# Gelu straight from PSUM in the second phase, and a block's first products behind all reads of their tile

## Chip, cores and metric

The kernel runs on one core of a Trainium2 chip. The metric is the device time of one execution in microseconds. Before the change three runs took 1274.23, 1276.29 and 1277.38 us (median 1276.29).

## The reference

For 8 batches of 576 tokens with model width 512 three things follow one another, all in float32. First, attention in chunks of 64 tokens with 8 heads of 64. Second, a feed-forward layer with a residual; third, a gated layer that mixes tokens:

```python
x = x + relu(layernorm(x, eps=1e-6) * g_ln @ w_ch1) @ w_ch2          # 512 -> 2048 -> 512
h = gelu_tanh(x @ w_in)                                              # 512 -> 1024
u, v = h[..., :512], h[..., 512:]
v_n = (v - mean(v)) / sqrt(var(v) + 1e-6) * g_ln
v_s = einsum('ts,bsd->btd', w_sg, v_n) + b_sg[None, :, None]         # 576 x 576 over tokens
out = x + (u * v_s) @ w_out
```

Gelu is `0.5 * h * (1 + tanh(c * (h + 0.044715 * h**3)))`.

## The kernel before

The 4608 tokens are 36 tiles of 128. A float32 product is made of three float16 products: each operand is split into a high and a low half, scaled by a power of two, and low times low is left out.

**First phase: attention and the feed-forward layer.** Its instructions are collected by a `Plan`. Every `op` names its engine, a planned duration, what it reads and writes (by keys such as `P1` or by buffers), a priority and a latency that its readers on other engines see. `Plan.run` then plays the engines against each other and emits the instructions in the order that comes out; on the chip each engine runs its own list in that order. The keys only set the order. What really waits for what is found out afterwards from the tiles that the emitted instructions touch.

Tokens go through the feed-forward layer in blocks of two tiles. From block 4 on (14 blocks) a block has eight steps j. `ff1p` makes the hidden units of a step on banks 2 and 3; `ff2p` multiplies them by the second matrix by a scheme with seven products, P1 to P7, each a sum over the eight steps. P1 and P6 lie in one bank of the two-bank tile `pair0`, P5 and P7 in its other bank, P2 and P3 in `bank6`, P4 in `bank7`. TensorE takes them in the order 1, 6, 5, 7, 2, 3, 4. The step behind a block's last hidden step is two `ff1p` later, so between the last products of a block and the first of the next lies one `ff1p` (24 matmuls). After the last step (`j == 7`) ScalarE copies P1 and P5, scaled, into the buffers `u`, VectorE evicts P6, P7, P2, P3 and P4, and POOL adds the parts together; then the block's two tiles are stored.

**Second phase: the gated layer.** It works by hand-written order, with four groups of nine tiles. A *unit* is one output tile of TensorE: `v_unit` (one token tile, 512 columns of v), `u_unit` (128 rows of u by 384 tokens), `s_unit` (the mixing over tokens), `o_unit` (a token tile of the output). Each takes the next of four PSUM banks:

```python
def nb():
    rot[0] += 1
    return bank[rot[0] % 4]
```

A unit first issues its matmuls, then `tick()`, which issues what earlier units have put off with `later(k, fn)`: `fn` is issued at the k-th tick from there. So gelu of unit n is spread: its first ScalarE passes and the first VectorE pass (L1024) are issued in unit n, the tanh at the tick of unit n+1, and the last VectorE pass (`last`, L1031) at the tick of unit n+2. For v, statistics, normalisation and the split into halves follow over further ticks.

Group 0 begins with its nine v_units, followed by twelve u_units. For groups 0 to 2 the order is u_units, two sets of four s_units, and then this stage, which mixes the next group's v_units with this group's o_units:

```python
for c in "v0 v1 v2 v3 o0 v4 o1 v5 o2 v6 o3 v7 v8 o4 o5 o6 o7 o8".split():
```

In the same stage the gated u is split into halves (`split`, L247 to L249), and its scale is found by a maximum over all partitions (`fin_g`, `turn`, `spread`).

Of the kernel before, what the change touches and what calls it, by code (L numbers as in the profile page):

```python
# [10 lines left out]
F32 = mybir.dt.float32  # L11
# [4 lines left out]
ALU = mybir.AluOpType  # L16
# [116 lines left out]
def fused_kernel(ctx: ExitStack, tc, qkv, w1, w2, g1, w_in, w_out, wsgt, wsgs, g2, b_sg, out):  # L133
# [38 lines left out]
    e2g, i2g = (small.tile([P, 4], F32, name=f"{n}2g") for n in "ei")  # L172
    g1s = small.tile([P, 4], F32, name="g1s")
# [500 lines left out]

    def ff2p(b, j):
# [19 lines left out]
        for p in (1, 6, 5, 7, 2, 3, 4):  # L695
            op("PE", 326, lambda p=p: mm(p), rd=[h, f"w2_{j}"], wr=[f"P{p}"] + extra, prio=1000 + nff[0])
        if j == 7:
# [8 lines left out]
            def stt(p, c, out, add, n=0):  # L706
                op("DVE", 480, lambda: nc.vector.scalar_tensor_tensor(  # L707
                    out=out(), in0=POS[p][0], scalar=c, in1=add(), op0=ALU.mult, op1=ALU.add
                ), rd=[f"P{p}", f"P{3 if p == 2 else p}"], wr=u if n else [x1 if p == 4 else x0], prio=-120, lat=1200)

            def copy(p, c, n):
                op("ACT", 380, lambda: nc.scalar.activation(
                    out=U(n), in_=POS[p][0], func=AF.Copy, scale=c
                ), rd=[f"P{p}", f"P{p + 5 if p == 1 else 7}"], wr=[u[n // 2]], prio=-120, lat=1200 if n else 300)

            def add(x, d, v, ns):
                op("POOL", ns, lambda: nc.gpsimd.tensor_tensor(  # L717
                    out=d(), in0=d(), in1=v(), op=ALU.add
                ), rd=u, wr=[x], prio=-50)

            copy(1, ca, 0)
            stt(6, cb, lambda: U(1), lambda: U(0), 1)
            copy(5, cb, 2)
            stt(7, cb, lambda: U(3), lambda: U(1), 3)
            stt(2, ca, lambda: half(x0, 0), lambda: half(x0, 0))
            stt(3, ca, lambda: half(x0, 1), lambda: half(x0, 1))
            stt(4, cn, lambda: half(x1, 0), lambda: half(x1, 0))
            add(x0, lambda: x0.t, lambda: u[0].t, 1250)
            add(x1, lambda: half(x1, 0), lambda: U(3), 700)
            add(x0, lambda: half(x0, 1), lambda: U(2), 700)  # L730
            add(x1, lambda: half(x1, 1), lambda: U(3), 700)
            add(x1, lambda: half(x1, 1), lambda: U(2), 700)
# [102 lines left out]
    def x2_cols(g0, n):  # L835

        e, inv = e2g[:, g0:g0 + n], i2g[:, g0:g0 + n]
        top2(e, inv)
        nc.vector.tensor_scalar_mul(inv, inv, 2.0 ** 14)
        nc.vector.tensor_scalar(out=e, in0=e, scalar1=col("win_c"), scalar2=None, op0=ALU.mult)  # L840

# [30 lines left out]
    with tc.manual_schedule():  # L872
# [144 lines left out]
        def gelu(g, ps, n, o, done=None):  # L1017

            h = pb.tile([P, 512], F32, tag="h", name="h", bufs=4)[:, :n]
            q = pb.tile([P, 512], F32, tag="q", name="q", bufs=4)[:, :n]  # L1020
            nc.scalar.activation(out=h, in_=ps, func=AF.Copy, scale=e2g[:, g:g + 1])
            nc.scalar.activation(out=q, in_=h, func=AF.Square, scale=GA)  # L1022
            tick()
            nc.vector.scalar_tensor_tensor(out=q, in0=q, scalar=1.0, in1=h, op0=ALU.add, op1=ALU.mult)  # L1024

            def tanh():
                nc.scalar.activation(out=q, in_=q, func=AF.Tanh, scale=GC)
                later(1, last)

            def last():  # L1030
                nc.vector.scalar_tensor_tensor(out=o, in0=q, scalar=1.0, in1=h, op0=ALU.add, op1=ALU.mult)  # L1031
# [5 lines left out]
        def v_unit(g, i):  # L1037
# [9 lines left out]
            def stats():  # L1047
# [7 lines left out]
                    out=rs, in0=mv[:, 1:2], scalar1=z, scalar2=4e-6 * z, op0=ALU.mult, op1=ALU.add  # L1055
# [37 lines left out]
        def s_unit(g, e, m):  # L1093
# [48 lines left out]
            def fin_g3():  # L1142
# [6 lines left out]
                    out=col(f"c5_{e}"), in0=e_, scalar1=col("wout_c"), scalar2=None, op0=ALU.mult  # L1149
# [132 lines left out]
```

## Time and profile before

| | before |
|---|---|
| median of 3 runs | 1276.29 us |
| profiled execution | 1274.01 us |
| its span, first to last instruction | 1272.2 us |
| TensorE busy | 1218.5 us (96%) |
| VectorE busy | 825.1 us (65%) |
| ScalarE busy | 586.5 us (46%) |
| POOL busy | 491.2 us (39%) |
| mean granted TensorE clock | 0.993 |

The second phase begins at 867 us. A timeline names the tiles by the program's names: `pair` is `pair0`, `pb` one of the second phase's banks, `u` the buffers of the block's end. "Idle before" is the time that the engine stood still ahead of an instruction, with what ended it. An instruction of VectorE or ScalarE may start a little before the one ahead has ended, so starts that follow each other are closer than the durations.

### The profile page before, as it was taken

Reading aid. Unit: us, or ns where it says so; the run is one execution under the profiler, and the core shown is the slowest. Engines: PE = TensorE matmul, PEld = TensorE weight load, DVE = VectorE, ACT = ScalarE, POOL = GpSimd, SP = SyncE. Lnnn points to the kernel's source line nnn. Section 1 sums busy time; section 2 is a strip of 40 time slices with the busy share of each in tenths; the row PEclk is TensorE's granted clock in tenths of the full one; section 3 lists DMA queues with packets and bytes.
Section 4 is the critical chain, followed back from the end, with each engine's and each line's share of the span. In section 5 each row is a group of like instructions: output and inputs, shape, how many; then the busy total and the mean of one; then the engine's idle time right before and its main releaser. Section 6 shows DMA issues by size and latency. Waiting matters only on the chain.

```text
span 1272.2 us, 26588 instructions
## 1 busy us (share of the span) xinstructions
PE 1218.5 (96%) x11119; PEld 872.5 (69%) x11119; DVE 825.1 (65%) x1621; ACT 586.5 (46%) x963; POOL 491.2 (39%) x446
## 2 busy tenths in 40 slices
PE   6889999988999999999999999999999999999998
PEld 4677654667888888888888888884544554554553
DVE  7885125995766656555555665546979579669665
ACT  5775402545834533333334333535736626526530
POOL 3341401644656544434444344233434144233220
PEclk9999999989999999999999999999999999999999
DMA  9954002246312221222132120612030331331102
GB/s 303 261 172 120 1 26 67 74 149 181 101 51 68 51 73 48 66 67 67 52 67 60 51 59 18 156 28 91 9 68 33 116 59 42 125 59 42 50 1 75
DMA packets 106392, 102.05 MB, mean 80 GB/s; under 512 B 79648, under 2 KB 79648, under 8 KB 106272
## 3 DMA queue, kind: packets, MB, share of 16 engines
q1 hardware_dynamic: 106272, 100.36, 28.2%
q8 instruction: 87, 1.43, 0.5%
q14 instruction: 33, 0.27, 0.1%
HBM read 62.59 MB, written 18.87 MB: 64 GB/s over the span
## 4 chain that ended last, share of the span: by engine, by line
PE 75%; DVE 14%; ACT 3%; DMA 3%; POOL 2%; issue 2%; SPq 0%; DVEq 0%; ACTq 0%; POOLq 0%
PE bank L640 20%; PE pair L689 11%; PE bank L689 8%; PE pb L1105 8%; PE pb L1087 7%; PE pb L1167 6%; PE pair L557 3%; PE pb L1043 3%; PE bank L536 3%; PE bank L557 2%; DMA straw<-in_w 2%; DVE gl L249 1%; PE pair L295 1%; DVE tf L600 1%; PE pb L1106 1%
## 5 line engine op out<-in xcount | busy, mean ns | idle before, releaser
L640 PE MATMUL bank<-xT,w1h 128*128 128x256 f16 x1792 | 301.6, 273 | 0.0
L689 PEld LDWEIGHTS <-arena 128*128 128x128 f16 x2352 | 226.7, 98 | 46.0 <-issue 17.0
L640 PE MATMUL bank<-xT,w1l 128*128 128x256 f16 x896 | 245.0, 273 | 0.0
L669 POOL TENSOR_TENSOR arena<-arena 128x896 f16<-128x896 f32 x69 | 130.2, 1886 | 255.6 <-ACT arena L667 255.5
L667 ACT ACTIVATE arena<-arena 128x896 f16<-128x896 f32 x112 | 106.3, 949 | 204.7 <-PE bank L689 131.4
L640 PEld LDWEIGHTS <-w1h 128*128 128x128 f16 x1792 | 175.3, 98 | 21.7 <-issue 0.5
L662 DVE TENSOR_TENSOR arena<-arena 128x256 f32<-128x256 f32 x112 | 63.6, 568 | 149.1 <-ACT arena L655 146.9
L655 ACT ACTIVATE arena<-bank 128x512 f32<-128x512 f32 x112 | 66.6, 595 | 123.7 <-PE bank L640 122.5
L689 PE MATMUL pair<-w2s,arena 128*128 128x256 f16 x672 | 110.6, 274 | 10.3 <-DVE u L707 6.8
L689 PE MATMUL pair<-w,arena 128*128 128x256 f16 x672 | 111.0, 274 | 2.7 <-DVE u L707 1.3
L1119 POOL TENSOR_TENSOR uT<-uT,vs 128x512 f32<-128x512 f32 x32 | 49.0, 1533 | 151.6 <-DVE vs L1115 151.6
L1043 PE MATMUL pb<-win,x2T 128*128 128x512 f16 x432 | 96.8, 379 | 1.5 <-DVE x L707 1.5
L640 PEld LDWEIGHTS <-w1l 128*128 128x128 f16 x896 | 87.9, 98 | 10.4
L1087 PE MATMUL pb<-x2T,win 128*128 128x384 f16 x576 | 94.6, 326 | 0.0
L689 PE MATMUL bank<-w,arena 128*128 128x256 f16 x672 | 93.7, 274 | 0.0
L536 PE MATMUL bank<-xT,w1h 128*128 128x256 f16 x512 | 86.1, 273 | 6.7 <-DVE latel L541 2.9
L1105 PE MATMUL pb<-wsg,vh 128*128 128x512 f16 x288 | 88.0, 380 | 0.0
L1167 PE MATMUL pb<-wout,gh 128*128 128x512 f16 x288 | 85.7, 379 | 1.9 <-DVE x L1172 1.9
L1087 PEld LDWEIGHTS <-win 128*128 128x128 f16 x576 | 56.2, 98 | 37.5
L717 POOL TENSOR_TENSOR x<-x,u 128x256 f32<-128x256 f32 (+1 forms) x60 | 64.4, 1089 | 44.3 <-ACT arena L667 30.8
L1024 DVE SCALAR_TENSOR_TENSOR q<-q,h 128x384 f32<-128x384 f32 (+1 forms) x84 | 51.3, 614 | 39.0 <-ACT q L1022 39.0
L1043 PEld LDWEIGHTS <-x2T 128*128 128x128 f16 x432 | 41.3, 98 | 50.9 <-issue 2.7
(225 smaller groups left out, 2332.5 us busy)
## 6 DMA issues: line engine op xcount, KB each, us to landing
straw<-in_w SPq DMA_DIRECT2D x16, 1023.8 KB, 6.6
qkl<-in_qkv SPq DMA_DIRECT2D x26, 512.0 KB, 3.8
x2d<-x SPq DMA_DIRECT2D x36, 256.0 KB, 2.0
x<-x2d SPq DMA_DIRECT2D x36, 256.0 KB, 4.4
out<-x SPq DMA_DIRECT2D x36, 256.0 KB, 2.0
vl<-in_qkv SPq DMA_DIRECT2D x26, 256.0 KB, 2.7
qk<-in_qkv SPq DMA_DIRECT2D x10, 512.0 KB, 5.7
raw<-in_w_in SPq DMA_DIRECT2D x4, 1023.8 KB, 5.6
```

What stands on the lines that cost most here:

```text
L536: nc.tensor.matmul(acc, lhsT=w[j][:, k, fc], rhs=xT.t[:, x, k], start=(n == 0), stop=(n == 11))
L557: nc.tensor.matmul(acc[i], lhsT=h[x].t[:, c], rhs=w2t[j][:, f % 2, y], start=(f == 0 and n == 0), stop=(f == NF - 1 and n == 2),)
L640: nc.tensor.matmul(acc[:, y * 256:y * 256 + 256], lhsT=w[j][:, k, fc], rhs=xT.t[:, x, k], start=(n == 0), stop=(n == 11),)
L655: op("ACT", 600, lambda: nc.scalar.activation(out=o.t[:, 0:4].rearrange("p n t -> p (n t)"), in_=acc, func=AF.Relu, scale=0.5), rd=[kb] + ...
L667: op("ACT", 950, lambda: nc.scalar.activation(out=h.t[:, 0], in_=o.t[:, 1:8], func=AF.Copy), rd=[o] + ar, wr=[h], prio=-100)
L669: op(lo[0], lo[1], lambda: lo[2].tensor_tensor(out=h.t[:, 1], in0=o.t[:, 1:8], in1=h.t[:, 0], op=ALU.subtract), rd=[o], wr=[h], prio=-100)
L689: nc.tensor.matmul(acc, lhsT=h.t[:, x, n], rhs=r(y), start=(first and j == 0 and m == 0), stop=(j == 7 and m == 2), skip_group_check=True,)
L717: op("POOL", ns, lambda: nc.gpsimd.tensor_tensor(out=d(), in0=d(), in1=v(), op=ALU.add), rd=u, wr=[x], prio=-50)
L1043: nc.tensor.matmul(ps, lhsT=x[:, k, c], rhs=w[:, k, 512:1024], start=(n == 0), stop=(n == 11))
L1087: nc.tensor.matmul(ps, lhsT=w[:, k, fc], rhs=x[:, k, c], start=(n == 0), stop=(n == 11))
L1105: nc.tensor.matmul(ps, lhsT=v[:, fc], rhs=w[:, 0:512], **f)
L1167: nc.tensor.matmul(ps, lhsT=x[:, k, c], rhs=w[:, k], start=(n == 0), stop=(n == 11))
```

## The change

In the first phase the first products of a new block take the tile's other products as written too (`OWN`), for `j == 0`. The reads at the block's end get keys of their own (`q1`, `q6`, `q7`, `q5`), the eviction of P7 stands ahead of the copy of P5 and no longer behind it, planned latencies of 1200 ns are dropped to the default, and planned durations of the copies and of POOL's additions are raised.

In the second phase gelu no longer makes a scaled copy `h` of the products in SBUF. Square, the first VectorE pass and the last one read the bank `ps` itself. The scale of h moves into columns: `eg` holds, for each group, the scales of Square and tanh and the eps of the layer norm, which five more small operations in `x2_cols` work out, and the scale that u has kept goes into the column `c5` of the output.

```diff
--- before.py
+++ after.py
@@ -170,6 +170,7 @@
     diag = small.tile([4, 4], F32, name="diag")
     redg = small.tile([P, 4], F32, name="redg")
     e2g, i2g = (small.tile([P, 4], F32, name=f"{n}2g") for n in "ei")
+    eg = small.tile([P, 3, 4], F32, name="eg")
     g1s = small.tile([P, 4], F32, name="g1s")
     g2s = small.tile([P, 4], F32, name="g2s")
     bb = small.tile([P, S], F32, name="bb")
@@ -672,6 +673,8 @@
 
         return rest
 
+    OWN = {1: ["P6", "P5", "P7"], 2: ["P3"]}
+
     def ff2p(b, j):
 
         nff[0] += 1
@@ -693,7 +696,7 @@
 
         extra = ["pair0", "bank7", "scr0", "scr1", "scr2"] if (b, j) == (B0, 0) else []
         for p in (1, 6, 5, 7, 2, 3, 4):
-            op("PE", 326, lambda p=p: mm(p), rd=[h, f"w2_{j}"], wr=[f"P{p}"] + extra, prio=1000 + nff[0])
+            op("PE", 326, lambda p=p: mm(p), rd=[h, f"w2_{j}"], wr=[f"P{p}"] + extra + OWN.get(p, []) * (j == 0), prio=1000 + nff[0])
         if j == 7:
             x0, x1 = x_t.pop(2 * b), x_t.pop(2 * b + 1)
 
@@ -703,33 +706,33 @@
 
             U = lambda n: u[n // 2].t[:, n % 2 * 256:n % 2 * 256 + 256]
 
-            def stt(p, c, out, add, n=0):
+            def stt(p, c, out, add, x, rd=()):
                 op("DVE", 480, lambda: nc.vector.scalar_tensor_tensor(
                     out=out(), in0=POS[p][0], scalar=c, in1=add(), op0=ALU.mult, op1=ALU.add
-                ), rd=[f"P{p}", f"P{3 if p == 2 else p}"], wr=u if n else [x1 if p == 4 else x0], prio=-120, lat=1200)
-
-            def copy(p, c, n):
-                op("ACT", 380, lambda: nc.scalar.activation(
+                ), rd=[f"P{p}", *rd], wr=[x], prio=-120)
+
+            def copy(p, c, n, rd, wr):
+                op("ACT", 470, lambda: nc.scalar.activation(
                     out=U(n), in_=POS[p][0], func=AF.Copy, scale=c
-                ), rd=[f"P{p}", f"P{p + 5 if p == 1 else 7}"], wr=[u[n // 2]], prio=-120, lat=1200 if n else 300)
+                ), rd=rd, wr=wr, prio=-120)
 
             def add(x, d, v, ns):
                 op("POOL", ns, lambda: nc.gpsimd.tensor_tensor(
                     out=d(), in0=d(), in1=v(), op=ALU.add
-                ), rd=u, wr=[x], prio=-50)
-
-            copy(1, ca, 0)
-            stt(6, cb, lambda: U(1), lambda: U(0), 1)
-            copy(5, cb, 2)
-            stt(7, cb, lambda: U(3), lambda: U(1), 3)
-            stt(2, ca, lambda: half(x0, 0), lambda: half(x0, 0))
-            stt(3, ca, lambda: half(x0, 1), lambda: half(x0, 1))
-            stt(4, cn, lambda: half(x1, 0), lambda: half(x1, 0))
-            add(x0, lambda: x0.t, lambda: u[0].t, 1250)
-            add(x1, lambda: half(x1, 0), lambda: U(3), 700)
-            add(x0, lambda: half(x0, 1), lambda: U(2), 700)
-            add(x1, lambda: half(x1, 1), lambda: U(3), 700)
-            add(x1, lambda: half(x1, 1), lambda: U(2), 700)
+                ), rd=u + ["q6", "q5", "q7"], wr=[x], prio=-50)
+
+            copy(1, ca, 0, ["P1", "P6"], u + ["q1"])
+            stt(6, cb, lambda: U(1), lambda: U(0), "q6", ["q1"])
+            stt(7, cb, lambda: U(3), lambda: U(1), "q7", ["q6"])
+            copy(5, cb, 2, ["P5", "P7", "q1"], ["q5"])
+            stt(2, ca, lambda: half(x0, 0), lambda: half(x0, 0), x0, ["P3"])
+            stt(3, ca, lambda: half(x0, 1), lambda: half(x0, 1), x0)
+            stt(4, cn, lambda: half(x1, 0), lambda: half(x1, 0), x1)
+            add(x0, lambda: x0.t, lambda: u[0].t, 1400)
+            add(x1, lambda: half(x1, 0), lambda: U(3), 850)
+            add(x0, lambda: half(x0, 1), lambda: U(2), 850)
+            add(x1, lambda: half(x1, 1), lambda: U(3), 850)
+            add(x1, lambda: half(x1, 1), lambda: U(2), 850)
             for t, x in ((2 * b, x0), (2 * b + 1, x1)):
                 done2(t, x)
 
@@ -838,6 +841,13 @@
         top2(e, inv)
         nc.vector.tensor_scalar_mul(inv, inv, 2.0 ** 14)
         nc.vector.tensor_scalar(out=e, in0=e, scalar1=col("win_c"), scalar2=None, op0=ALU.mult)
+        for k, y in enumerate((GA, GC)):
+            nc.vector.tensor_scalar_mul(eg[:, k, g0:g0 + n], e, y)
+
+        z = eg[:, 2, g0:g0 + n]
+        nc.vector.reciprocal(z, e)
+        nc.vector.tensor_tensor(out=z, in0=z, in1=z, op=ALU.mult)
+        nc.vector.tensor_scalar_mul(z, z, 4e-6 * 2.0 ** (-2 * VK))
 
     def x2_hi(g, i):
         hl = x2p[0].tile([P, 2, D], F16, tag="x2hl", name="x2hl", bufs=2)
@@ -1016,19 +1026,17 @@
 
         def gelu(g, ps, n, o, done=None):
 
-            h = pb.tile([P, 512], F32, tag="h", name="h", bufs=4)[:, :n]
             q = pb.tile([P, 512], F32, tag="q", name="q", bufs=4)[:, :n]
-            nc.scalar.activation(out=h, in_=ps, func=AF.Copy, scale=e2g[:, g:g + 1])
-            nc.scalar.activation(out=q, in_=h, func=AF.Square, scale=GA)
+            nc.scalar.activation(out=q, in_=ps, func=AF.Square, scale=eg[:, 0, g:g + 1])
             tick()
-            nc.vector.scalar_tensor_tensor(out=q, in0=q, scalar=1.0, in1=h, op0=ALU.add, op1=ALU.mult)
+            nc.vector.scalar_tensor_tensor(out=q, in0=q, scalar=1.0, in1=ps, op0=ALU.add, op1=ALU.mult)
 
             def tanh():
-                nc.scalar.activation(out=q, in_=q, func=AF.Tanh, scale=GC)
+                nc.scalar.activation(out=q, in_=q, func=AF.Tanh, scale=eg[:, 1, g:g + 1])
                 later(1, last)
 
             def last():
-                nc.vector.scalar_tensor_tensor(out=o, in0=q, scalar=1.0, in1=h, op0=ALU.add, op1=ALU.mult)
+                nc.vector.scalar_tensor_tensor(out=o, in0=q, scalar=1.0, in1=ps, op0=ALU.add, op1=ALU.mult)
                 if done:
                     done()
 
@@ -1052,7 +1060,7 @@
                 nc.vector.bn_aggr(out=mv, in_=bs)
                 z = 2.0 ** (-2 * VK)
                 nc.gpsimd.tensor_scalar(
-                    out=rs, in0=mv[:, 1:2], scalar1=z, scalar2=4e-6 * z, op0=ALU.mult, op1=ALU.add
+                    out=rs, in0=mv[:, 1:2], scalar1=z, scalar2=eg[:, 2, g:g + 1], op0=ALU.mult, op1=ALU.add
                 )
                 nc.gpsimd.tensor_tensor(out=rs, in0=rs, in1=cpow, op=ALU.pow)
                 later(2, lambda: norm(mv, rs))
@@ -1146,7 +1154,7 @@
                 top2(e_, inv)
                 nc.vector.tensor_scalar_mul(sg, inv, 2.0 ** 14)
                 nc.vector.tensor_scalar(
-                    out=col(f"c5_{e}"), in0=e_, scalar1=col("wout_c"), scalar2=None, op0=ALU.mult
+                    out=col(f"c5_{e}"), in0=e_, scalar1=col("wout_c"), scalar2=e2g[:, g:g + 1], op0=ALU.mult, op1=ALU.mult
                 )
                 r = slice(64 * e, 64 * e + 64)
                 nc.vector.tensor_copy(col("c5_m")[r], col(f"c5_{e}")[r])
```

## Rows read from the trace of the kernel before

**Rows 1.** TensorE's waits: line, awaited, us in total, times, longest.

```profile
PE pair L689 <- DVE u L707: 8.1, 12, 1.0
...
PE pair L689 <- ACT u L712: 3.0, 4, 1.8
...
PE pb L1167 <- DVE x L1172: 1.9, 3, 0.6
...
PE pb L1043 <- DVE x L707: 1.5, 1, 1.5
...
PE pair L689 <- ACT x L712: 1.1, 2, 0.6
...
PE pair L689 <- DVE x L707: 0.6, 1, 0.6
```

**Rows 2.** Timeline, block boundary: start, us, engine, line, operation, out<-in, count, [idle before].

```profile
481.17 0.48 DVE L707 SCALAR_TENSOR_TENSOR u<-pair,c_c2b,u 128x256 f32<-128x256 f32 x1 [0.33 <-PE pair L689]
...
482.88 0.46 ACT L712 ACTIVATE u<-pair,c_c2b 128x256 f32<-128x256 f32 x1
...
484.50 0.49 PE L689 MATMUL pair<-w,arena 128*128 128x256 f16 x3
...
485.10 0.48 DVE L707 SCALAR_TENSOR_TENSOR u<-pair,c_c2b,u 128x256 f32<-128x256 f32 x1 [1.00 <-PE pair L689]
...
485.64 0.49 PE L689 MATMUL pair<-w2s,arena 128*128 128x256 f16 x3 [0.65 <-DVE u L707]
```

**Rows 3.** Windows: stretch, length, busy PE PEld DVE ACT POOL, clock, DMA, GB/s.

```profile
891.10:914.60 23.50, 23.50 (x146) 14.17 (x145) 21.75 (x39) 20.43 (x41) 12.40 (x14) 1.00 0.00 1
945.70:991.30 45.60, 44.70 (x208) 19.99 (x206) 42.84 (x80) 26.50 (x44) 20.18 (x26) 1.00 0.16 47
```

**Rows 4.** Timeline of TensorE, stage of v_units and o_units (v3, v5, o3).

```profile
951.26 2.76 PE L1043 MATMUL pb<-win,x2T 128*128 128x512 f16 x12
...
962.04 2.75 PE L1043 MATMUL pb<-win,x2T 128*128 128x512 f16 x12
...
970.62 0.59 PE L1167 MATMUL pb<-wout,gh 128*128 128x512 f16 x2 [0.64 <-DVE x L1172]
```

**Rows 5.** Timeline of VectorE, same stage (a split; last passes, v0, v2 to v4).

```profile
954.09 0.82 DVE L249 SCALAR_TENSOR_TENSOR gl<-uT,c_sg,gh 128x576 f16<-128x576 f32 x1 [1.27 <-ACT gh L248]
...
955.03 0.67 DVE L1031 SCALAR_TENSOR_TENSOR gv<-q,h 128x512 f32<-128x512 f32 x1
...
960.78 0.69 DVE L1031 SCALAR_TENSOR_TENSOR gv<-q,h 128x512 f32<-128x512 f32 x1
...
967.25 0.68 DVE L1031 SCALAR_TENSOR_TENSOR gv<-q,h 128x512 f32<-128x512 f32 x1
...
971.64 0.68 DVE L1031 SCALAR_TENSOR_TENSOR gv<-q,h 128x512 f32<-128x512 f32 x1
```

**Rows 6.** Groups by line and shape: count, busy us, mean ns, idle before.

```profile
L1024 DVE SCALAR_TENSOR_TENSOR q<-q,h 128x512 f32<-128x512 f32 x36 | 24.6, 690 | 2.3 <-ACT q L1022 2.3
...
L1115 DVE SCALAR_TENSOR_TENSOR vs<-pb,c_c,bb 128x512 f32<-128x512 f32 x32 | 23.8, 744 | 6.6 <-PE pb L1105 4.6 <-PE pb L1106 1.4
...
L1148 DVE TENSOR_SCALAR c_c<-c_g_e,c_wout_c 128x1 f32<-128x1 f32 x8 | 1.6, 204 | 0.0
```

**Rows 7.** Groups by line, shapes together: gelu's scaled copy.

```profile
L1021 ACT ACTIVATE h<-pb,e2g 128x384 f32<-128x384 f32 (+1 forms) x84 | 52.0, 619 | 43.7 <-PE pb L1087 32.3 <-PE pb L1043 11.4
```

**Rows 8.** Timelines, v stage of group 0: u_units on TensorE, u1's last pass.

```profile
891.09 5.20 PE L1087 MATMUL pb<-x2T,win 128*128 128x384 f16 x31
...
904.29 1.51 DVE L1031 SCALAR_TENSOR_TENSOR uT<-q,h 128x384 f32<-128x384 f32 x1
```

**Rows 9.** Timeline of TensorE, attention in the first phase.

```profile
272.31 0.69 PE L295 MATMUL pair<-qkl 64*64 64x64 f32 x32 [2.63 <-DVE x L344]
```

**Rows 10.** Windows after two waits of TensorE.

```profile
273.00:276.40 3.40, 3.40 (x18) 2.39 (x18) 3.33 (x9) 0.00 (x0) 0.74 (x2) 0.51 1.02 116
300.20:303.70 3.50, 3.46 (x32) 3.11 (x32) 3.47 (x9) 2.39 (x4) 0.36 (x1) 1.00 0.58 176
```

## The prediction

> **What bounds the kernel now.** I read four views, in this order. The page's first two parts say that TensorE is busy in 96% of the span and near full in every slice after the first, so a microsecond is won only where TensorE waits and lost only where it is made to wait. The list of TensorE's waits [rows 1] then shows how little there is to win. At the block boundaries of the first phase the products of L689 wait 8.1 + 0.6 us for VectorE's evictions (13 waits, one per boundary) and 3.0 + 1.1 us for ScalarE's copies; the second phase adds 1.5 us at its start and 1.9 us in three places. The timeline of one boundary [rows 2] shows what the 13 waits are. The new block's P1 products start at 484.50, straight behind the fc1 matmuls. Only then, at 485.10, comes the old block's last read of the same tile (the P7 eviction), and the new P6 products wait for it until 485.64, for 0.65 us. A later write waits for every read of `pair0` issued before it, and a later read for every write, whichever quarter they touch.
>
> For the second phase I took busy time by stage [rows 3]. In the 45.6 us in which v_units and o_units alternate, TensorE is busy 44.7 us, but VectorE 42.8 us too, and ScalarE only 26.5 us. The reader is to see that VectorE has no room there. TensorE's timeline [rows 4] and VectorE's [rows 5] of that stage, laid side by side, show that VectorE runs far behind: v5 starts on TensorE at 962.04, while VectorE writes v3's last gelu pass at 967.25, though v3's products were done by 954.0. Today nobody minds, because v3's bank was freed by ScalarE's copy.
>
> **The change part by part.** *First phase, own tiles and order.* P1 of a new block is now planned behind the reads of P1, P6, P5 and P7, and the P7 eviction no longer behind the P5 copy. In [rows 2] the P6 eviction runs at 481.17 and the P5 copy from 482.88 to 483.34; with the P7 eviction (0.48 us) next to the P6 one, all reads are over by about 483.9 even if each waits for the other, 0.6 us ahead of the new P1 at 484.50. So the wait goes and nothing on TensorE takes its place: -8.7 us over 13 boundaries. The other 4.1 us stay: they are the old block's P5 or P7 behind the copy of P1, whose position the change leaves alone. At the phase change the P7 eviction was the last of VectorE's five and held the first v_unit for 1.5 us; it now comes second or later. If the new bank waits for that tile alone, up to 1.4 us go, if for all five evictions nothing; I take -0.7 us. Together -9.4 us; bounds -12 us (part of the copy waits goes too) and 0 (the attention matmuls that cover the copy of P1 at most boundaries shift, and 0.6 us appear where 0.65 us went). The POOL costs of 1400 and 850 are planner numbers only.
>
> *Second phase, ScalarE.* 84 copies of 0.619 us go [rows 7], 52 us of ScalarE's time, and Square takes over their PSUM operand and their column scale, so I price it like the copy. With ScalarE at 26.5 of 45.6 us this is off the path, but for one place: VectorE's gap of 1.27 us at 954.09 [rows 5], in which it waits for a ScalarE output queued behind v2's copy. One copy less there, with the tanh ahead of it still tied to VectorE, gives about 0.5 us back.
>
> *Second phase, VectorE.* Both gelu passes now read PSUM. The trace has the same operation either way: 690 ns from SBUF, 744 ns with one PSUM operand [rows 6], so +0.054 us for each of 168 passes, 9.1 us of VectorE's time. [...] Five one-column operations are added to `x2_cols`, twice; the nearest row is 204 ns [rows 6], issued about 0.19 us apart: +0.95 us in the v stage of group 0, hidden in the first phase at the other call. The eps column on POOL I cost at nothing (bounds -0.1 and +0.1 us of POOL, idle over half of the stage).
>
> *Second phase, the banks: the large term.* A unit's bank is one of four in rotation, so unit n+4 needs bank n. Before, ScalarE's copy freed it at once. Now it is freed by the last of the three passes, a VectorE instruction issued two ticks later. The order is v0 v1 v2 v3 o0 v4 o1 v5 o2 v6 o3 ..., so o0 needs v0's last pass, v4 v1's, o1 v2's, and v5 v3's. By [rows 5] these end at 955.7 for v0, 961.5 for v2 and 967.9 for v3. TensorE wants the banks earlier: v3 starts at 951.26 and its 12 matmuls run 0.216 us apart (2.76 less one matmul of 0.38, over 11), 2.59 us a unit, so o0 could start at 953.9, and v5 starts at 962.04 [rows 4].
> The worst is v5. VectorE's schedule up to v3's last pass moves by -0.5 us (the gap) and by five dearer passes ahead of it (v2's and v3's first, v0's, v1's and v2's last: +0.27 us) to start at 967.0; it takes 0.73 us, so it ends at about 967.8, and TensorE starts 0.06 us after a release (as at 485.64 in [rows 2]): 967.9, 5.8 us late. The stalls at o0 (some 1.5 us) and o1 (0.6 us) lie inside these 5.8 us. After v5 the banks come in time: v4's last pass, at 971.64 today [rows 5], ends near 972.2 and v6 starts at 967.9 + 2 x 2.59 = 973.1. o3 then starts at 975.7 in place of 970.62, and its own wait of 0.64 us is gone: +5.1 us for the stage. Bounds: VectorE idles only 2.8 us in the whole stage [rows 3], so it can't be more than that earlier: +2.6 us at least; without the gap regained, +5.6 us. Three such stages (groups 0 to 2): +15.2 us.
> Group 0's v stage has no o_units, but VectorE is as full: 21.8 of 23.5 us [rows 3], and slowest in the same way. u1's last pass starts at 904.29 and takes 1.51 us, beside a POOL subtraction [rows 8]: end 905.8. u5 needs that bank and starts today at 891.09 + 5 x 1.95 = 900.85 (u_unit: 12 matmuls 0.163 us apart). VectorE gets there later by the 0.95 us of `x2_cols` and by 16 dearer passes, 0.86 us, or earlier by 1.0 us if the POOL overlap doesn't recur: u5 starts between 906.7 and 907.7. +6.2 us (5.8 to 6.9). The u_units behind it come in time: VectorE does two passes for each, some 0.65 us apiece, in 1.95 us, and catches up. So do s_units, and the u_units of group 3.
>
> *The clock.* In the wait ahead of v5 TensorE stands for about 3.9 us in one piece. [...] I take a fall for each of the three long waits: 3.4 us at half speed hold back 1.7 us of matmuls, and no later bank wait absorbs it (v6 has 0.9 us to spare, o3 5). +5.1 us, bounds 0 and 5.1. In group 0 the longest piece is 2.2 us, followed by further bank waits that would swallow a fall: 0.
>
> **Sum.** -9.4 + 15.2 + 6.2 + 5.1 = +17.1 us. The profiled execution took 1274.01 us (span 1272.2 us and 1.8 us around it), so 1291.1 us; the median of the runs shown is 2.3 us above it, and so is my forecast: 1293 us.
>
> **The rivals.**
> *The clock does not fall* (or only once or twice). [...] +12.0 us: 1288 us.
> *The first phase gives nothing*: P1 now waits for four reads on two engines instead of one, and where ScalarE is behind its plan that wait returns, or the copy of P1 loses its cover. For it: the list has a boundary at which TensorE waited 1.8 us for ScalarE [rows 1]. Against it: 0.6 us to spare at the regular boundary. 0 in place of -9.4 us: 1302 us.
> *The lag of VectorE shrinks*, since a stall gives it time and its POOL overlaps fall elsewhere: by the lower bound 2.6 us a stage, 4 in group 0, no fall: 11.8 - 9.4 = +2.4 to +8: 1279 to 1284 us.
> *No bank is late*, the other side: freed of 52 us, ScalarE feeds VectorE earlier, the last passes end in time, and the first phase's 9.4 us are all that is left: 1267 us. It decides at v3: its last pass must end before 962.0, 5.8 us sooner than worked out, and about as much in group 0. For it: one of ScalarE's three passes per unit goes. Against it: VectorE waits for ScalarE or POOL in only 2.8 us of the stage.
> *The banks are not held*, because the planned tiles differ from what the code says: no, `gelu` reads `ps` itself in its last pass, and `nb` still rotates four.
>
> **How the numbers follow.** Forecast 50%, clock steady 20%, first phase nothing 12%, lag shrinks 11%, no late bank 7%. The range 1280 to 1303 us leaves out the last, and part of the lag case. A change of 0.3% is 3.8 us, about what a measurement of this kernel can tell from none: slower by more, 88%; within, 5% (the low end of the lag case); faster, 7%.
>
> **What would show it.** Right: in TensorE's waits, L1043 and L1167 behind the second pass over `ps` (VectorE, the old L1031) with about 1.5, 0.6 and 4 us in each of the three stages, and L1087 of group 0 with some 5 us in pieces; granted clock near 0.5 after v5's wait; L689 without its 0.65 us waits but with some 4 us behind the copy; VectorE's passes near 745 ns at 512 columns. Wrong: no such waits with VectorE's last pass of v3 ahead of v5, waits of L689 behind the P5 copy, or VectorE's order in the stage not that of [rows 5].

## The result and the profile after

The changed kernel takes 1288.49 us (median of 4 runs, 1287.76 to 1290.72) against 1275.26 us (1273.49 to 1277.38) for the kernel before on the same chip: a ratio of 1.0106, 95% interval 1.0084 to 1.0128, slower by 13.2 us where 17 were forecast. The profiled execution's span grew from 1272.2 to 1287.0 us, by 14.8 us.

Cut the span where the second phase's first product starts (866.95 us before, 859.75 us after), at the small product (L207, in `turn`) that lies ahead of v3 in each of the three v-and-o stages, and at the first such product of the last group. That gives -7.2 us for the first phase with the phase change, then +4.1 us for group 0, +4.6, +5.9 and +7.4 us from one cut to the next, each with one stage's waits, and 0.0 for the rest: a second phase of 427.3 in place of 405.3 us.

The page first: its span, its busy times and the granted clock in 40 slices.

```profile
span 1287.0 us, 26597 instructions
...
PE 1223.5 (95%) x11119; PEld 873.1 (68%) x11119; DVE 838.4 (65%) x1631; ACT 549.7 (43%) x879; POOL 477.0 (37%) x446
...
PEclk9999999989999999999999999999999999998999
```

The same 11119 matmuls are busy for 1223.5 us where they took 1218.5 before, at a mean granted clock of 0.989 where it was 0.993, so part of the loss is clock, not waiting. ScalarE lost 37 us of work, and the kernel did not gain by it. TensorE's waits, to be read against [rows 1] (line, awaited, us in total, times, longest). L692 is the feed-forward products, L1051 the v_units, L1175 the o_units, L1095 the u_units:

```profile
PE pb L1051 <- DVE gv L1039: 11.1, 3, 3.7
...
PE pair L692 <- ACT u L715: 5.1, 9, 0.6
...
PE pb L1175 <- DVE gv L1039: 3.4, 3, 1.1
...
PE pb L1051 <- DVE x L710: 2.0, 1, 2.0
PE pb L1095 <- DVE gv L1039: 1.7, 2, 1.4
...
PE pair L692 <- ACT x L715: 1.1, 2, 0.6
...
PE pb L1095 <- DVE uT L1039: 0.2, 1, 0.2
```

The 8.1 + 0.6 us behind VectorE in the first phase are gone. The waits behind ScalarE's copy grew from 4.1 to 6.2 us. Four lines are new, all behind L1039, gelu's last pass over the bank: 16.4 us. Now the stage of [rows 4], on TensorE: u4 of group 0, the first o_unit, and v5 in each of the three stages.

```profile
895.80 15.76 PE L1095 MATMUL pb<-x2T,win 128*128 128x384 f16 x96 [0.19 <-DVE uT L1039]
...
952.08 0.59 PE L1175 MATMUL pb<-wout,gh 128*128 128x512 f16 x2 [1.15 <-DVE gv L1039]
...
964.34 2.75 PE L1051 MATMUL pb<-win,x2T 128*128 128x512 f16 x12 [3.69 <-DVE gv L1039]
...
1069.17 4.06 PE L1051 MATMUL pb<-win,x2T 128*128 128x512 f16 x12 [3.70 <-DVE gv L1039]
...
1175.31 5.28 PE L1051 MATMUL pb<-win,x2T 128*128 128x512 f16 x12 [3.70 <-DVE gv L1039]
```

The same wait three times over, but the 12 matmuls behind it take 2.75, 4.06 and 5.28 us. VectorE in that stage, against [rows 5]: u1's last pass in group 0 with the POOL subtractions beside it, the shrunken gap, and the last passes of v0, v2 and v3.

```profile
895.66 2.45 POOL L1077 TENSOR_TENSOR vl<-gv,vh 128x512 f16<-128x512 f32 x2
...
897.02 0.54 DVE L1039 SCALAR_TENSOR_TENSOR uT<-q,pb 128x384 f32<-128x384 f32 x1
...
950.43 0.82 DVE L250 SCALAR_TENSOR_TENSOR gl<-uT,c_sg,gh 128x576 f16<-128x576 f32 x1 [0.70 <-ACT gh L249]
...
951.36 0.67 DVE L1039 SCALAR_TENSOR_TENSOR gv<-q,pb 128x512 f32<-128x512 f32 x1
...
957.16 0.68 DVE L1039 SCALAR_TENSOR_TENSOR gv<-q,pb 128x512 f32<-128x512 f32 x1
...
963.62 0.68 DVE L1039 SCALAR_TENSOR_TENSOR gv<-q,pb 128x512 f32<-128x512 f32 x1
```

Read the two fences together: v0's pass ends at 952.03 and the o_unit starts at 952.08; v3's pass ends at 964.30 and v5 starts at 964.34. The release is the pass, each time. The groups by line and shape (busy us, mean ns, idle before) show what a pass costs, against [rows 6, 7]:

```profile
L1035 ACT ACTIVATE q<-q,eg 128x512 f32<-128x512 f32 x36 | 25.5, 715 | 28.5 <-DVE q L1032 28.4
L1030 ACT ACTIVATE q<-pb,eg 128x512 f32<-128x512 f32 x36 | 24.6, 684 | 47.6 <-PE pb L1051 47.3
L1039 DVE SCALAR_TENSOR_TENSOR gv<-q,pb 128x512 f32<-128x512 f32 x36 | 24.4, 677 | 0.0
L1032 DVE SCALAR_TENSOR_TENSOR q<-q,pb 128x512 f32<-128x512 f32 x36 | 24.1, 670 | 10.7 <-ACT q L1030 10.6
...
L1123 DVE SCALAR_TENSOR_TENSOR vs<-pb,c_c,bb 128x512 f32<-128x512 f32 x32 | 23.9, 746 | 11.2 <-PE pb L1113 9.5 <-PE pb L1114 1.7
...
L1039 DVE SCALAR_TENSOR_TENSOR uT<-q,pb 128x384 f32<-128x384 f32 x48 | 26.5, 552 | 0.5 <-ACT q L1035 0.5
```

With a PSUM operand VectorE's passes take 670 and 677 ns, not the 744 I had priced. The last pass of u became cheaper; the same group before:

```profile
L1031 DVE SCALAR_TENSOR_TENSOR uT<-q,h 128x384 f32<-128x384 f32 x48 | 31.5, 657 | 0.0
```

Now the timeline of a block boundary, against [rows 2]:

```profile
473.51 0.69 PE L315 MATMUL pair<-vl,pt 64*64 64x64 f32 x32
474.14 0.50 PE L692 MATMUL pair<-w,arena 128*128 128x256 f16 x3
...
475.33 0.47 ACT L715 ACTIVATE u<-pair,c_c2a 128x256 f32<-128x256 f32 x1 [1.06 <-PE pair L692]
475.86 0.49 PE L692 MATMUL pair<-w2s,arena 128*128 128x256 f16 x3 [0.56 <-ACT u L715]
...
477.48 0.48 DVE L710 SCALAR_TENSOR_TENSOR u<-pair,c_c2b,u 128x256 f32<-128x256 f32 x1 [0.54 <-ACT u L715]
...
479.78 0.49 PE L692 MATMUL pair<-w,arena 128*128 128x256 f16 x3
480.11 0.49 PE L692 MATMUL pair<-w2s,arena 128*128 128x256 f16 x3
```

The P7 eviction is over at 477.96, 1.8 us ahead of the new block's P1 at 479.78, and the P6 products behind it no longer wait. But the old block's P7 products now wait 0.56 us for the copy of P1. Before, attention products ran beside that copy, between the old block's P6 and P5 products:

```profile
479.60 0.69 PE L314 MATMUL pair<-vl,pt 64*64 64x64 f32 x32
479.71 0.47 ACT L712 ACTIVATE u<-pair,c_c2a 128x256 f32<-128x256 f32 x1
```

The phase change:

```profile
856.92 0.48 DVE L710 SCALAR_TENSOR_TENSOR x<-pair,c_c2b,x 128x256 f32<-128x256 f32 x1 [2.38 <-PE pair L692]
...
857.44 0.47 ACT L715 ACTIVATE x<-pair,c_c2b 128x256 f32<-128x256 f32 x1 [1.17 <-DVE x L710]
857.95 0.48 DVE L710 SCALAR_TENSOR_TENSOR x<-pair,c_c2b,x 128x256 f32<-128x256 f32 x1 [0.54 <-ACT x L715]
...
859.13 0.47 DVE L710 SCALAR_TENSOR_TENSOR x<-bank,c_c2a,x 128x256 f32<-128x256 f32 x1
...
859.75 3.57 PE L1051 MATMUL pb<-win,x2T 128*128 128x512 f16 x9 [1.96 <-DVE x L710]
```

The first product of the second phase waits for the last of VectorE's five evictions (859.60). Last the granted clock, where a *fall* is a stretch in which the granted clock is near 0.5, behind the long waits (stretch, length, busy PE, PEld, DVE, ACT, POOL, clock, DMA, GB/s), against [rows 10]:

```profile
964.34:967.10 2.76, 2.76 (x13) 1.27 (x13) 2.73 (x6) 0.72 (x1) 1.68 (x3) 1.00 0.00 0
1069.17:1073.23 4.06, 4.06 (x13) 1.57 (x13) 3.99 (x8) 0.72 (x1) 1.94 (x3) 0.67 0.15 58
1175.45:1180.50 5.05, 5.05 (x13) 1.78 (x12) 4.60 (x9) 0.72 (x1) 1.94 (x3) 0.50 0.15 55
859.75:863.15 3.40, 3.40 (x10) 1.24 (x11) 0.51 (x1) 0.00 (x0) 3.40 (x5) 0.57 0.02 5
```

A clock of 1.00 after the first of the three, part and then all of the stretch near 0.5 after the second and third (0.67 and 0.50), and a fall behind the phase change (0.57) that I had not expected.

### The profile page after: what moved, and what is told of

Its sections match the earlier page's. It is cut to its first block, busy times and chain, and to the rows that moved or that the text cites. A ratio compares the mean times of both kernels' runs of the same rounds, so it can differ in the third digit from the quotient of the medians.

```text
span 1287.0 us, 26597 instructions
## 1 busy us (share of the span) xinstructions
PE 1223.5 (95%) x11119; PEld 873.1 (68%) x11119; DVE 838.4 (65%) x1631; ACT 549.7 (43%) x879; POOL 477.0 (37%) x446
## 4 chain that ended last, share of the span: by engine, by line
PE 77%; DVE 13%; DMA 3%; ACT 3%; POOL 1%; issue 1%; SPq 0%; DVEq 0%; ACTq 0%; POOLq 0%
PE bank L641 20%; PE pair L692 11%; PE bank L692 8%; PE pb L1113 8%; PE pb L1095 7%; PE pb L1175 6%; PE pb L1051 5%; PE pair L558 3%; PE bank L537 3%; PE bank L558 2%; DMA straw<-in_w 2%; DVE gl L250 1%; PE pair L296 1%; DVE tf L601 1%; PE pair L315 1%; PE pb L1114 1%
## 5 line engine op out<-in xcount | busy, mean ns | idle before, releaser
L692 PEld LDWEIGHTS <-arena 128*128 128x128 f16 x2352 | 228.2, 98 | 36.6 <-issue 8.1
L663 DVE TENSOR_TENSOR arena<-arena 128x256 f32<-128x256 f32 x112 | 71.3, 637 | 105.7 <-ACT arena L656 105.6
L692 PE MATMUL pair<-w2s,arena 128*128 128x256 f16 x672 | 110.7, 274 | 6.2 <-ACT u L715 5.1
L1051 PE MATMUL pb<-win,x2T 128*128 128x512 f16 x432 | 102.3, 395 | 13.0 <-DVE gv L1039 11.1
L692 PE MATMUL pair<-w,arena 128*128 128x256 f16 x672 | 111.1, 274 | 0.1
L1030 ACT ACTIVATE q<-pb,eg 128x384 f32<-128x384 f32 (+1 forms) x84 | 52.5, 624 | 110.6 <-PE pb L1095 62.9
L1095 PE MATMUL pb<-x2T,win 128*128 128x384 f16 x576 | 95.1, 326 | 1.9 <-DVE gv L1039 1.7
L692 PE MATMUL bank<-w,arena 128*128 128x256 f16 x672 | 91.7, 273 | 0.0
L1175 PE MATMUL pb<-wout,gh 128*128 128x512 f16 x288 | 86.0, 380 | 3.6 <-DVE gv L1039 3.4
L1051 PEld LDWEIGHTS <-x2T 128*128 128x128 f16 x432 | 42.6, 101 | 66.8 <-issue 21.8
L1095 PEld LDWEIGHTS <-win 128*128 128x128 f16 x576 | 56.2, 98 | 40.0 <-issue 2.6
L1032 DVE SCALAR_TENSOR_TENSOR q<-q,pb 128x384 f32<-128x384 f32 (+1 forms) x84 | 50.6, 603 | 49.6 <-ACT q L1030 49.4
```

Source lines behind the costliest of these rows:

```text
L663: nc.vector.tensor_tensor(out=two(6, 8), in0=two(1, 3), in1=two(0, 2), op=ALU.subtract)
L692: nc.tensor.matmul(acc, lhsT=h.t[:, x, n], rhs=r(y), start=(first and j == 0 and m == 0), stop=(j == 7 and m == 2), skip_group_check=True,)
L1051: nc.tensor.matmul(ps, lhsT=x[:, k, c], rhs=w[:, k, 512:1024], start=(n == 0), stop=(n == 11))
L1095: nc.tensor.matmul(ps, lhsT=w[:, k, fc], rhs=x[:, k, c], start=(n == 0), stop=(n == 11))
L1175: nc.tensor.matmul(ps, lhsT=x[:, k, c], rhs=w[:, k], start=(n == 0), stop=(n == 11))
```

## The experiments

Medians are each beside the kernel before on the same chip. "Second phase" is the length from its first product to the end of the span in the profiled execution, 405.3 us before and 427.3 us after; it leaves out the first phase's own scatter.

**The two halves apart.** `e1` is the kernel before with the first-phase part alone, `e2` the kernel before with the gelu part alone.

```diff
# e1: before, plus OWN, stt, copy and add as in the change
# e2: before, plus eg, x2_cols and gelu as in the change
```

> The first-phase part alone; gelu and everything behind it as before. Theory H (the bank is held too long, and that is the whole loss): the second phase starts some 7 us earlier, as it does with the full change, loses 0.4 us and a clock fall of 1.7 us at the phase change, and is otherwise as before: about 1270 us (1267 to 1271), 5 us under the kernel before. Rival P (the loss is the price of the three passes, wherever it falls) says the same of this run. A theory by which the first phase's gain only shifts a wait into the second phase expects no change, 1275 us.

Measured: 1266.01 against 1273.15 us, 0.9947 (0.9927 to 0.9967), -7.1 us.

> The second-phase part alone; the first phase as before. Theory H: what the second phase lost in the changed kernel's trace without the clock fall at the phase change, 22.0 - 1.7 = +20 us over the kernel before: 1295 us (1292 to 1298). If the two parts only lose together (the first phase's new end sets off the second phase's waits), less than +10 us: below 1285.

Measured: 1294.75 against 1273.15 us, 1.0170 (1.0153 to 1.0187), +21.6 us; second phase 427.4 us. The two add up to +14.5 us, which agrees with the change's 13.2 within the intervals. The first part gains, the second costs three times as much.

**Is it the bank or the passes?** Both kernels put a copy back (without scale) and leave one of VectorE's passes on PSUM: in `e3` the last one, in `e4` the first.

```diff
+ h = pb.tile([P, 512], F32, tag="h", name="h", bufs=4)[:, :n]
+ nc.scalar.activation(out=h, in_=ps, func=AF.Copy)
+ nc.scalar.activation(out=q, in_=h, func=AF.Square, scale=eg[:, 0, g:g + 1])
...
# e3: first pass in1=h,  last pass in1=ps
# e4: first pass in1=ps, last pass in1=h
```

> The changed kernel with the copy to SBUF back (ScalarE copies ps to h, Square and the first VectorE pass read h); only the last VectorE pass still reads the bank. So the hold is the same, one PSUM pass in place of three, and ScalarE's copy is back. Theory H: the waits ahead of o0 and v5 are as in the changed kernel (1.2 and 3.7 us): 1288 us (1285 to 1292). Rival P: two of three PSUM reads are gone, so at least half of the second phase's loss goes: 1278 us or less.

Measured: 1292.16 against 1273.15 us, 1.0147 (1.0125 to 1.0168), +19.0 us; second phase 432.6 us. Its waits of TensorE behind gelu (v_units, o_units, u_units):

```profile
PE pb L1053 <- DVE gv L1041: 11.1, 3, 3.7
...
PE pb L1177 <- DVE gv L1041: 5.5, 3, 1.8
...
PE pb L1097 <- DVE gv L1041: 2.6, 3, 2.0
```

> The twin of the run that only holds: copy back as there, but now the first VectorE pass reads the bank and the last one reads h, so the bank is free one tick and a half earlier. Instruction count and PSUM reads are equal in both. Theory H: from the trace before, v3's first pass ends at 959.4, ahead of v5's start at 962.0, but v4's at 969.5, 2.2 us behind v6's start; so some 2 us a stage are left, nothing in group 0: 1270 + 6 = 1276 us (1272 to 1279). Rival P: same reads, same time as the run that only holds.

Measured: 1271.17 against 1273.15 us, 0.9994 (0.9978 to 1.0010), -2.0 us; second phase 412.3 us. Its waits behind gelu:

```profile
PE pb L1053 <- DVE q L1034: 6.5, 3, 2.2
```

With ScalarE's copy back but the bank held to the last pass, every wait of the changed kernel returns, and at o0 a longer one. With the bank released one pass earlier the 3.7 us waits go; what is left is 2.2 us at v6 and 0.3 us in group 0. So the cost is when the bank is released, not how many passes read PSUM.

**More banks.** The three-pass gelu stays and the rotation grows from four banks to five, then to seven.

```diff
- return bank[rot[0] % 4]
+ return bank[rot[0] % 5]                     # e5
...
+ i = next(i for i in lru if i in free)       # e6, e6b: least recently used
+ lru.remove(i); lru.append(i); return bank[i]
...
# e6:  v_, u_, o_units of banks 0-4, 6, 7; s_units of 0-4
# e6b: v_, o_units of banks 0-4, 6, 7; u_, s_units of 0-4,
#      and an s_unit puts the bank of its tail last in lru
```

> The changed kernel with a rotation of five banks (the eighth bank of PSUM, which no tile uses in the second phase, joins). Theory H: unit n+5 needs bank n, so v3's last pass now meets o2, one unit later than v5; from the changed kernel's trace (last pass ends at 964.3, o2 would start at 961.4 without waits) a wait of some 2.9 us a stage is left, none ahead of o0 and o1, none in group 0. Against the kernel before: 0 us (-2 to +4, with or without clock falls). Rival P (price of the passes): +13 us as the changed kernel.

Measured: 1274.43 against 1272.43 us, 1.0017 (1.0005 to 1.0030), +2.0 us; second phase 414.8 us.

```profile
PE pb L1175 <- DVE gv L1039: 7.9, 3, 2.6
```

One bank more takes the waits at v5, o0 and group 0 away and leaves one of 2.64 us per stage, now at o2, close to the 2.9 expected. Two of the three drew a fall behind them: from o2's start to the next unit's it took 4.27 and 3.96 us in the first and third stage, 2.59 in the second.

> The changed kernel with seven banks to choose from, least recently used first (v_, u_ and o_units from 0 to 4, 6 and 7, s_units from 0 to 4; before four). Theory H: no unit waits for a bank any more, the o_units' 0.64 us neither; the second phase is as long as before less 2 us, and the first phase's gain remains: 9 us under the kernel before (-6 to -11). Rival P: VectorE's passes cost as they do in the changed kernel, +10 us or more. A theory by which the full VectorE bounds the stage whatever the banks expects +5 us or more.

Measured: 1275.42 against 1272.43 us, 1.0032 (1.0014 to 1.0049), +3.0 us. A miss of mine in building it: the u_units were given the banks in which the s_units keep their tails, so parts of u are overwritten in it, and new waits of 0.5 to 2.5 us came up there (4.0 us at the s_units' first products, 3.8 us at v0). It says nothing on the question. `e6b` keeps the tails' banks from the u_units.

> The changed kernel with seven banks for v_units and o_units (0 to 4, 6 and 7), while u_units and s_units take theirs from 0 to 4, so that no unit writes the bank of the s_units' tails before they are read. Theory H: no unit waits for a bank, the o_units' 0.64 us neither: 9 us under the kernel before (-6 to -11). If the full VectorE bounds the stage whatever the banks: no gain over five banks, 2 us over the kernel before.

Measured: 1266.45 against 1272.40 us, 0.9948 (0.9931 to 0.9966), -6.0 us; second phase 405.1 us, of which 1.7 us are the fall behind the phase change. Of its waits at the first products of units in the second phase two are left:

```profile
PE pb L1053 <- DVE x L710: 2.0, 1, 2.0
...
PE pb L1097 <- DVE uT L1041: 0.2, 1, 0.2
```

With enough banks the three passes cost nothing, though VectorE is nearly as busy in the second phase as before (294 us of it, 301 before). From four to seven banks the second phase gives back 22.2 us (427.3 to 405.1), all that the change had lost in it.

**The clock by itself.** 32 products into an unused bank are put ahead of v5, where TensorE stood; the wait itself stays. If the falls come because TensorE stands, they go, and with them the 1.3 + 2.8 us that they cost in the second and third stage: some 9 us over the kernel before. If they come whatever TensorE does, the time stays.

```diff
+ if g and i == 5:
+     for _ in range(32):
+         nc.tensor.matmul(bank[4][:, 0:256], lhsT=wouth[:, 0, 0:128], rhs=wouth[:, 0, 0:256], start=True, stop=True)
```

> The changed kernel with 32 extra matmuls (128x256, f16, into the unused bank, read by nobody) ahead of v5 in each of the three stages, 3.5 us of work in the 3.7 us in which TensorE stands there. [...] Rival (the falls are the chip's own, whatever TensorE does there): falls as before and +13 us or more.

Measured: 1282.47 against 1272.43 us, 1.0082 (1.0062 to 1.0102), +10.0 us; second phase 421.5 us. v5 in the second and third stage:

```profile
1065.94 2.75 PE L1054 MATMUL pb<-win,x2T 128*128 128x512 f16 x12 [0.21 <-DVE gv L1039]
...
1170.78 2.75 PE L1054 MATMUL pb<-win,x2T 128*128 128x512 f16 x12 [0.21 <-DVE gv L1039]
```

In place of 4.06 and 5.28 us v5 takes 2.75, and no fall came in the three stages (clock 1.00 over v5 in each). Without the filling, seven of eight waits of 3.7 us were followed by one: two of three in the changed kernel, two in `e3` and three in `e9`. The second phase is 5.8 us shorter than the changed kernel's, and the changed kernel's falls add up to 1.7 + 1.3 + 2.8 = 5.8 us. The fall behind the phase change did not come in this run either, although its wait of 1.96 us was there; that 1.7 us of the 5.8 is not the filling's doing.

**The copy of P1.** `e8` is `e1` with the copy of P1 planned behind the old block's P5 and P7 products.

```diff
- copy(1, ca, 0, ["P1", "P6"], u + ["q1"])
+ copy(1, ca, 0, ["P1", "P6", "P5", "P7"], u + ["q1"])
```

> The first-phase part alone (gelu as before), with one more step: the copy of P1 is planned behind P5 and P7 of its block as well, so that no product of the block is issued behind it. Theory: the 11 waits of 0.56 us behind the copy (6.2 us) go; the block's reads end some 0.7 us later, still 0.3 us or more ahead of the next block's first products. 6 us under the run with the first-phase part alone, 13 us under the kernel before. Rival: the reads are then late for the next block's first products, and 0.5 us waits return there: no better than the first-phase part alone, 7 us under the kernel before.

Measured: 1259.73 against 1272.43 us, 0.9905 (0.9888 to 0.9922), -12.7 us, 5.6 more than `e1`. Its waits at the second phase's start and at block boundaries:

```profile
PE pb L1045 <- DVE x L709: 2.1, 1, 2.1
...
PE pair L691 <- DVE u L709: 1.3, 1, 1.3
```

The 6.2 us behind the copy are gone, one wait of 1.3 us behind VectorE is left. The second phase starts at 852.91 instead of 859.93 us.

**Is a PSUM operand dear in another slot?** The changed kernel's passes read PSUM as the second tensor, the row I had priced them by [rows 6] as the first. `e9` exchanges the operands; the `+1` of both passes is left out, so what it computes is not gelu.

```diff
- out=q, in0=q, scalar=1.0, in1=ps, op0=ALU.add, op1=ALU.mult
+ out=q, in0=ps, scalar=1.0, in1=q, op0=ALU.mult, op1=ALU.mult
...
# the last pass alike
```

> The changed kernel with the operands of both VectorE passes exchanged: the bank as first tensor input, q as second. The operation is then (ps * 1) * q; the +1 of both passes is left out, so gelu is not computed, at an equal count of operations. Theory S (a PSUM operand costs VectorE time as first input only): the passes at 512 columns take 744 ns, as L1115 before, in place of 670 and 677; the wait ahead of v5 grows by some 0.5 us a stage, group 0 by 1 to 2 us: 3 us over the changed kernel, 16 us over the kernel before. Rival (the 744 ns belong to the other operands of L1115 and L1172, not to the slot): 675 ns, time as the changed kernel, +13 us.

Measured: 1289.17 against 1272.40 us, 1.0128 (1.0110 to 1.0146), +16.8 us.

```profile
L1039 DVE SCALAR_TENSOR_TENSOR gv<-pb,q 128x512 f32<-128x512 f32 x36 | 24.5, 680 | 0.0
L1032 DVE SCALAR_TENSOR_TENSOR q<-pb,q 128x512 f32<-128x512 f32 x36 | 24.3, 674 | 9.3 <-ACT q L1030 9.2
```

Theory S falls, although its time fitted: the passes take 674 and 680 ns in either slot. The waits in the second phase are the changed kernel's to 0.02 us, and the second phase takes 427.2 us against 427.3: the falls came behind v5 in all three stages here and not at the phase change. The medians of the two kernels are 0.7 us apart; the rest of the difference between +16.8 and +13.2 us is the kernel before, 1272.40 us beside `e9` and 1275.26 beside the changed kernel. The time alone would have told the wrong story.

**Both fixes together.** `e10` is the changed kernel with seven banks, the later copy of P1, and in the last block the copy of P5 behind the P7 eviction. `e11` is the same with the gelu of the kernel before.

> All steps together with the three-pass gelu: first-phase part, copy of P1 planned behind P7, in the last block the copy of P5 behind the eviction of P7 (VectorE then does its five evictions without waiting for ScalarE: 0.54 us off the wait at the phase change, 2.1 to 1.6 us), and seven banks. From the runs so far: -12.7 (copy behind) - 1.9 (o_units) - 0.5 to -2.2 (phase change, with a clock fall if it goes too): 15 to 17 us under the kernel before, 1257 us on this scale. If the three passes cost something that the banks hid: behind the twin with the old gelu by more than 2 us.

Measured: 1254.66 against 1272.40 us, 0.9860 (0.9839 to 0.9881), -17.7 us; second phase 403.3 us.

```profile
PE pb L1053 <- DVE x L710: 1.8, 1, 1.8
```

> The twin with the old gelu (scaled copy), all else equal: first-phase part, copy of P1 behind P7, last block's order, seven banks. The o_units' waits of 0.64 us go here too. 15 to 17 us under the kernel before. Against its twin: VectorE's passes cost the same from either memory (690 and 680 against 670 and 677 ns) and ScalarE is not full, so both agree within 2 us.

Measured: 1255.93 against 1272.40 us, 0.9869 (0.9853 to 0.9884), -16.5 us; second phase 402.9 us. Both beat the kernel before and the changed one. The twins' second phases agree within 0.4 us and their intervals overlap: once banks suffice, taking some 39 us off ScalarE gives nothing that can be told from none, since ScalarE bounded nothing.

## Why the prediction was right, point by point

The direction, the mechanism and the place were right: v5 waits for v3's last pass in each stage, for 3.7 us of the 3.9 worked out. The 17.1 us became 13.2 through sizes that partly cancel. In the profiled execution, to which the points below belong, it is 14.8: the first phase and the phase change gained 1.1 us less each than forecast, the stages and group 0 lost 1.4 and 3.8 us less, the clock cost 0.7 us more. That the total came this close is in part luck.

- **First phase, -8.7 us: measured -7.6.** Its last product ended at 857.80 in place of 865.43 us. The 13 waits went and nothing on TensorE replaced them at the new P1, as said. The step that failed is that the 4.1 us behind the copy of P1 stay: they became 6.2. At 479.60 before, attention products lay between the old block's products and covered the copy; they now run at 473.51, ahead of P1, and the copy stands bare. The waits of the feed-forward products thus fell by 6.6 us, not 8.7; the other 1.0 us lies elsewhere in the first phase and can't be told from scatter (in the traces of kernels with this same first phase the second begins between 856.56 and 860.15 us). The bounds named that case. `e8` shows the price: without these waits the same part gives 5.6 us more.
- **Phase change, -0.7 us: measured +0.4, and 1.7 us of clock.** The bound "if for all five evictions nothing" is what happened, and the P5 copy, now between the P6 and P7 evictions, delays the last one. The wait grew from 1.52 to 1.96 us, and v0 to v2 (36 matmuls) took 9.62 us where the same 36 take 7.93 in `e5`, `e7` and `e9`. I had charged no fall there.
- **Stage, +5.1 us each: measured +4.6** in the stage without a fall. o0 waits 1.15 us (1.5 predicted), v5 3.69 (3.9), o3's 0.64 us are gone. Of the 0.6 us at o1 only some 0.2 came: v2's last pass ends at 957.84, and o1 starts at 957.90, 0.45 us behind the product ahead of it, where 0.22 us is usual; the list of waits shows no row for it. Counted from start to start, o0, o1 and v5 lose 1.3, 0.2 and 3.8 us, and o3 regains 0.8: 4.6 us. The terms on either side of VectorE were off together: the gap shrank by 0.57 us (0.5 predicted), and the five dearer passes, +0.27 us, weren't dearer, so v3's last pass ended some 0.4 us sooner than worked out.
- **VectorE's price, +0.054 us a pass: measured 0 or less.** 670 and 677 ns against 690 and 680 from SBUF; all 168 passes together were busy for 101.5 us where they took 107.3 before. The term was mis-sized because the row I took differs from the pass in two things, the PSUM operand and a scalar that is a column; `e9` rules out the slot. The row that stays at 744 to 746 ns has a column scalar, and so has VectorE's operation of the same length on SBUF alone, with float16 for one input and the output (x2hl, L848 of the kernel before: median 742 ns over the 27 in the second phase). So the column, not PSUM, goes with the 60 to 70 ns; no kernel here changed the column alone, so the cause is not shown.
- **Group 0, +6.2 us: measured +2.4 without the fall.** The waits are 1.42, 0.33 and 0.19 us, at u2 to u4, and u5 comes in time. u1's last pass ends 11.98 us after the first u_unit's start (885.58 to 897.56) where it was 14.71 before [rows 8]: it took 0.54 us, not 1.51. I had said that this needs the overlap with POOL not to recur; it did recur (POOL's subtractions run from 895.66 to 898.11), and the pass, which now reads PSUM, was not slowed by it. The 0.86 us of dearer passes did not come, and the five operations in `x2_cols` added some 0.75 us to VectorE's list (0.95 predicted). The rest of the shorter lag lies in the traces. Ahead of u1's last pass three more operations of VectorE took 1.22 to 1.38 us beside POOL before; with u1's pass the four took 5.48 us, and now 2.71. The first pass of the stage also runs earlier without the copy ahead of it, by 0.66 us in `e9`, which has the same three waits and no fall. 2.8 + 0.7 - 0.75 us make up the 2.7 us.
- **The clock, +5.1 us for three falls: measured 0, 1.3 and 2.8 in the stages.** With the 1.7 us at the phase change the sum is 5.8, so it fits by luck in this kernel. The 1.7 us a fall were my estimate from [rows 9, 10]: a clock of 0.51 for 3.4 us behind the wait of 2.63 us, and of 1.00 behind the one of 1.76 us that ended at 300.24. That a wait of 3.7 us draws a fall held in seven of eight (the changed kernel, `e3`, `e9`), and this kernel has the one exception; how long the fall then lasts differs, below, and the fall at the phase change I had not forecast.
- **The rivals.** "No bank is late" decided by v3's last pass before 962.0 on the old time axis; shifted by the stage's 3.09 us that is 958.95, and the pass ended at 964.30. "The first phase gives nothing" fell (`e1`). "The lag shrinks" held in group 0 alone. "The clock does not fall" was the nearest in time, 1288 us, and yet not what the trace shows.

## What to carry to other kernels

A pass that read PSUM cost its own time here and also the bank until that pass ended (v5 started 0.04 us behind v3's pass); before taking a copy out, find the instruction that will now release the bank and where it stands in its engine's queue, and count banks by how many units that engine runs behind. In this case `e3` and `e4` show what a release one pass earlier is worth (20 us of the second phase), and `e6b` that more banks do as well. The 39 us of work taken off ScalarE, which bounded nothing here, were worth nothing that can be told from none, as the twins `e10` and `e11` show (1254.66 and 1255.93 us).

## What the runs showed of the hardware

- The same stop of TensorE did not always cost the same clock. Three waits of 3.69 to 3.70 us were followed by no fall, a short and a long one (clock 1.00, 0.67 and 0.50 over v5, which took 2.75, 4.06 and 5.28 us). In `e9` the same waits drew a fall all three times, with v5 at 5.28, 4.44 and 4.17 us, and in two stages of `e3`, with v5 at 4.44 and 5.28 us. The stops of 2.64 us in `e5` drew one in two of three stages (4.27 and 3.96 us over o2, 2.59 in the other), those of 2.18 us in `e4` in none (v6 took 2.75 us in each). The 1.96 us at the phase change drew one in five of nine kernels (9.62 us for 36 matmuls, as in the changed one, `e1` and `e6b`; 7.93 in `e5`, `e7` and `e9`).
- Gelu's passes on VectorE were not slowed by POOL once they read PSUM. Before, six of the 168 passes took 1.22 to 1.63 us, each beside a subtraction or product of POOL (others beside one were not slowed). After the change none took over 0.69 us, though five last passes of u lay wholly beside such an operation, at 0.54 to 0.56 us. The twins agree: the 48 last passes of u take 658 ns on average from SBUF in `e11` and 552 from PSUM in `e10`. The reason is not shown.
- Reads of one two-bank PSUM tile by two engines follow one another in this program: at the phase change the copy of P5 starts 0.04 us after the P6 eviction ends, and the P7 eviction 0.04 us after that copy. P6 and P5 lie in different banks and share the tile alone; the P5 copy and the P7 eviction also write the same buffer. Whether the chip or the program orders them is not shown.
- On ScalarE a scale from a column in place of a constant went with 90 to 95 ns more: tanh at 512 columns took 715 ns, 625 before; at 384 columns 605 and 510.
